# Attention and feed-forward kernel: 64-bit weight words rebuilt by three VectorE steps instead of four, with a scaled copy in an output bank

## The chip, the cores and the metric

The kernel runs on one core of one Trainium2 chip. The metric is the device time in microseconds of one execution; lower is better. Three runs of the kernel before gave 979.25, 982.62 and 982.91 us (median 982.62). A separate execution was taken with the hardware profiler; the views of the trace come from that one.

The engines are called as the profile calls them: PE is TensorE (matrix products), PEld its weight load, DVE is VectorE, ACT is ScalarE, POOL is GpSimd, SP is the engine that issues the DMA transfers. SBUF is the on-chip working memory, PSUM the memory into which PE accumulates.

## The reference

Two stages. The first is attention with a mask from hashes, over 4 batches of 8 heads, 768 positions and 64 dimensions. A position's hash is six bits, the signs of its product with `proj`; a query sees the keys of its own bucket. The second is a feed-forward layer over 3072 tokens, 512 wide inside and out, 2048 in the middle.

```python
q_bits = (np.einsum('bhsd,dk->bhsk', q, proj) > 0)
k_bits = (np.einsum('bhsd,dk->bhsk', k, proj) > 0)
mask = q_bucket[:, :, :, None] == k_bucket[:, :, None, :]
scores = np.where(mask, scale * np.matmul(q, k.transpose(0, 1, 3, 2)), -1000000000.0)
attn = np.exp(scores - np.max(scores, axis=-1, keepdims=True))
attn = attn / (np.sum(attn, axis=-1, keepdims=True) + 1e-09)
x = np.matmul(attn, v)              # then heads side by side: 3072 x 512
h = x @ w_in
g = np.where(h >= 1, h, np.where(h <= -1, 0.0, (h + 1) ** 2 / 4))
out = g @ w_out
```

The two weight matrices come as 64-bit floats. The kernel sees each number as two 32-bit words, a high one (sign, 11 exponent bits, 20 bits of the fraction) and a low one, and makes a 32-bit float of them on the chip.

## The kernel before, in words

**Precision.** Most products are made from a rounded high part and a low part (the difference), so that one product of the reference is three on PE. Names end in `h`/`hi` and `l`/`lo`.

**Attention: heads and units.** The 32 heads are worked through one behind the other in 384 *units* `g` (loop at line 614), twelve to a head (`NU`): two halves of the queries (`hf`) by six blocks of keys (`j`). In what follows a unit is counted within its head, 0 to 11; unit 12 is unit 0 of the next head. Heads go in pairs; an *even* head is the first of its pair, an *odd* one the second. Unit `g` issues, in this order:

- `s_unit(g)`: two products of 384 columns into one of four `s` banks of PSUM (lines 372, 373), then two exponentials on ACT: the rounded one into `ph` (381) and the full one (386), which goes back into the `s` bank, or into `pf` in SBUF where POOL will read it.
- in every second unit, `max_red` (line 315): DVE reduces the two `smax` banks, 768 numbers, to a maximum. There is one pair of such banks, so the next maximum's products wait for the reduce before.
- `lo_unit(g - 1)`: the low part `pl`, full less rounded (line 39, by the helper `sub`): on POOL for blocks 0 and 3, on DVE for the other four.
- `pv_unit(g - 4)`: three products (405, 407, 409) into the *output bank* `obank[hf]`. The four units of delay (`LAG`) mean that `obank[0]` collects in units 4 to 9 and `obank[1]` in units 10 to 15; ACT then copies the bank out (415). In the other six units a bank is idle.
- after every second unit, `max_mm` (311): two products for the maximum of a later head.
- the unit's *tasks*, from a table that is filled beforehand by `at(unit, function)`. Each engine takes its instructions in the order of issue.

**Tasks of a pair.** They prepare the pair that comes two pairs later: in units 0 to 3 of an even head POOL casts the raw rows (153) and makes their low parts (158, shown as line 39 with `t<-raw,t`), four pieces; DMA moves (`move`) copy parts to the other half of the partitions. In unit 3 POOL clamps the maxima (`max_clamp`, 343, 345), in unit 5 PE transposes them (`max_tr`, 350) and ACT copies them out (355). The hash bits are `bits_mm`, four products (211) per half of the positions into an output bank, ACT's negated copy of a part of them (217), and in the next unit `bits_cmp`, a comparison on DVE (222). They stand in units 7 (`obank[1]`) and 11 (`obank[0]`) of the even head, the third `move` behind the second one's comparison in unit 12, the scaling of the bits on POOL (274) in unit 13. V is cast on ACT in unit 6 and its low parts are made on POOL in units 7 and 9.

**Weights.** 32 slices of 128 x 512 numbers are rebuilt: 24 during attention, one per head from head 3 to head 26, and eight in the feed-forward stage. `WeightSplit.steps` returns a slice's steps, and `conv` puts them into the table of tasks with a list of units. `s0` loads the words. `s1` squares the high word, read as a float, on ACT (69) and takes its lower 27 bits shifted left by three on DVE (70); `s2` ors in the two top bits (74), `s3` the low word shifted right (78); `s4` multiplies with 1 or 0 by a test of the square, which makes tiny numbers zero (82). The units are 7, 9, 13 and 15, so that each head holds, on DVE, line 78 of the head before in its unit 1, line 82 in unit 3, and its own lines 70 and 74 in units 7 and 9. Later steps cast (87 or 89), subtract (39) and store.

**Sums.** In heads 8, 16 and 24 a batch is complete; three small DVE steps (673, 674, 678) prepare its sums in unit 11 of the following odd head and unit 5 of the even head behind.

**Feed-forward** begins near 461 us: for two chunks of 384 tokens, twelve products per step into `h` (966) and nine into `y` (829); then the other six chunks by products of half-size blocks (1061). ACT and DVE make the activation between (788 to 803). The eight remaining weight slices are rebuilt at the start of this stage, by a table of steps (lines 1218 to 1238).

Of the kernel before, what the change touches and what calls it, by code (L numbers as in the profile page):

```python
# [11 lines left out]
F32 = mybir.dt.float32  # L12
# [22 lines left out]
WMIN2 = float(np.array([897 << 20], np.int32).view(np.float32)[0]) ** 2  # L35
# [6 lines left out]
class WeightSplit:  # L42
# [3 lines left out]
    def __init__(self, nc, pool, n):  # L46
        self.nc, self.pool, self.n = nc, pool, n
        sc = pool.tile([P, 2], I32, name="wsc", bufs=1)
        nc.vector.memset(sc[:, 0:1], -0x40000000)
        nc.vector.memset(sc[:, 1:2], 29)  # L50
        self.sc = sc

    def steps(self, src, shape, hi, lo, cp, stage=None, low=None, keep=None):
# [10 lines left out]
        def s1():  # L64
            raw = st["raw"]
            sq = st["sq"] = self.pool.tile([P, n], F32, name="wsq")
            a = st["a"] = self.pool.tile([P, n], I32, name="wa", bufs=1)
            high = raw[:, :, 1].bitcast(F32)
            nc.scalar.activation(out=sq, in_=high, func=AF.Square)
            nc.vector.tensor_scalar(out=a, in0=raw[:, :, 1], scalar1=0x07FFFFFF, scalar2=3,  # L70
                                    op0=ALU.bitwise_and, op1=ALU.logical_shift_left)

        def s2():
            nc.vector.scalar_tensor_tensor(out=st["a"], in0=st["raw"][:, :, 1], scalar=self.sc[:, 0:1],
                                           in1=st["a"], op0=ALU.bitwise_and, op1=ALU.bitwise_or)

        def s3():
            nc.vector.scalar_tensor_tensor(out=st["a"], in0=st["raw"][:, :, 0], scalar=self.sc[:, 1:2],
                                           in1=st["a"], op0=ALU.logical_shift_right, op1=ALU.bitwise_or)

        def s4():
            nc.vector.scalar_tensor_tensor(out=st["sq"], in0=st["sq"], scalar=WMIN2,
                                           in1=st["a"].bitcast(F32), op0=ALU.is_ge, op1=ALU.mult)
# [13 lines left out]
        if stage is None:  # L97
            return [s0, s1, s2, s3, s4, s5, s6] + ([put] if keep is not None else [])
# [5 lines left out]
        return [s0, s1, s2, s3, s4, put], [get, s5, s6]  # L104
# [10 lines left out]
def attention(ctx, tc, wst, T1, T2, qk, v, pj, cv, x_d, s_d, e_d, tasks, shared):  # L115
# [4 lines left out]
    shared["work"], shared["small"] = work, small  # L120
# [450 lines left out]
    for hd in range(NH):  # L571
# [7 lines left out]
        if h == 0 and pr + 2 < NPAIR:  # L579
# [9 lines left out]
            bits_at = ((20, 1), (23, 0)) if pr == 0 else ((8 if pr == 1 else 7, 1), (11, 0))  # L589
# [516 lines left out]
def lsh_attn_ffn(ctx: ExitStack, tc: tile.TileContext, qk, v, pj, cv, w_in, w_out, out):  # L1106
# [49 lines left out]

    def wi_steps(i, cp, stage=None):
# [133 lines left out]
```

## Time and profile before

| | |
|---|---|
| three runs | 979.25, 982.62, 982.91 us |
| the profiled execution, its own time | 979.4 us |
| span of its trace, first to last instruction | 977.6 us |
| mean granted TensorE clock | 1.000 |
| busy share PE, PEld, DVE, ACT, POOL | 98%, 91%, 81%, 70%, 36% |
| DVE busy, 76.9 to 409.7 us (heads 4 to 27) | 312.25 of 332.80 us |
| PE busy, 461 to 969 us | 507.94 of 508.00 us |

How to read it. A busy share is an average over the span. PE's records overlap each other (a product of 384 columns is shown as some 0.34 us long while the next one starts 0.176 us behind it), so a busy PE may still be waiting; what counts is the distance from one start to the next. In the timeline a row has the start in us from the span's beginning, the duration in us, engine, line and operation, output and inputs by the program's names, the shape, how many instructions the row stands for, and in brackets how long the engine had been idle and which instruction released it. In the groups by line a row ends with the busy time in us and the mean duration in ns, then the idle time before them.

### The profile page before, as it was taken

Reading aid. Unit: us, or ns where it says so; the run is one execution under the profiler, and the core shown is the slowest. Engines: PE = TensorE matmul, PEld = TensorE weight load, DVE = VectorE, ACT = ScalarE, POOL = GpSimd, SP = SyncE. Lnnn points to the kernel's source line nnn. Section 1 sums busy time; section 2 is a strip of 40 time slices with the busy share of each in tenths; the row PEclk is TensorE's granted clock in tenths of the full one; section 3 lists DMA queues with packets and bytes.
Section 4 is the critical chain, followed back from the end, with each engine's and each line's share of the span. In section 5 each row is a group of like instructions: output and inputs, shape, how many; then the busy total and the mean of one; then the engine's idle time right before and its main releaser. Section 6 shows DMA issues by size and latency. Waiting matters only on the chain.

```text
span 977.6 us, 15547 instructions
## 1 busy us (share of the span) xinstructions
PE 961.9 (98%) x5050; PEld 890.3 (91%) x5050; DVE 788.3 (81%) x1355; ACT 680.2 (70%) x1481; POOL 354.8 (36%) x422
## 2 busy tenths in 40 slices
PE   8999999999999999999999999999999999999998
PEld 7889999999999999999999998888988888888896
DVE  8779999999999999897898788787776777655554
ACT  7888998989989998987755565455564545544444
POOL 8768887777788877566000000000000000000000
PEclk9999999999999999999999999999999999999999
DMA  5775566677666666635494479976459554454431
GB/s 161 191 183 157 153 170 177 175 191 197 179 167 166 157 175 176 153 114 134 128 335 162 139 227 300 295 241 201 119 160 236 146 183 118 148 154 119 119 87 65
DMA packets 95113, 167.56 MB, mean 171 GB/s; under 512 B 13956, under 2 KB 51960, under 8 KB 95032
## 3 DMA queue, kind: packets, MB, share of 16 engines
q1 hardware_dynamic: 94808, 166.56, 60.7%
q8 instruction: 40, 0.66, 0.3%
q14 instruction: 41, 0.34, 0.1%
q10 hardware_dynamic: 224, 0.00, 0.0%
HBM read 106.13 MB, written 33.87 MB: 143 GB/s over the span
## 4 chain that ended last, share of the span: by engine, by line
PE 86%; DVE 5%; POOL 5%; ACT 1%; issue 1%; DMA 1%; DVEq 0%; POOLq 0%; ACTq 0%
PE y L829 27%; PE h L1061 18%; PE h L966 7%; PE smax L311 6%; PE s L373 5%; PE s L372 5%; PE o L405 5%; PE o L407 5%; PE o L409 5%; POOL t L39 3%; PE o L211 2%; DVE nm L315 2%; DVE pl L39 1%; POOL pl L39 1%; POOL t L153 1%
## 5 line engine op out<-in xcount | busy, mean ns | idle before, releaser
L381 ACT ACTIVATE ph<-s 128x384 fp32r<-128x384 f32 x380 | 188.6, 496 | 41.2 <-PE s L373 36.1
L315 DVE TENSOR_REDUCE nm<-smax 128x1 f32<-128x768 f32 x189 | 179.3, 949 | 22.2 <-PE smax L311 21.0
L39 POOL TENSOR_TENSOR pl<-pf,ph 128x384 fp32r<-128x384 f32 x128 | 134.1, 1052 | 78.8 <-ACT pf L386 78.8
L794 DVE SCALAR_TENSOR_TENSOR t<-t 128x384 f32<-128x384 f32 x128 | 71.2, 557 | 101.0 <-ACT z L789 100.8
L39 DVE TENSOR_TENSOR pl<-s,ph 128x384 fp32r<-128x384 f32 x256 | 135.4, 545 | 10.9 <-ACT s L386 9.0
L372 PE MATMUL s<-t 128*128 128x384 f32 x384 | 132.2, 344 | 0.0
L373 PE MATMUL s<-t 128*128 128x384 f32 x384 | 129.6, 337 | 1.7 <-DMA t<-te 1.7
L409 PE MATMUL o<-pl,va 128*128 128x386 f32 x384 | 130.4, 340 | 0.4 <-DVE pl L39 0.4
L407 PE MATMUL o<-ph,vb 128*128 128x386 f32 x384 | 130.0, 339 | 0.0
L405 PE MATMUL o<-ph,va 128*128 128x386 f32 x384 | 129.9, 338 | 0.0
L386 ACT ACTIVATE s<-s 128x384 f32<-128x384 f32 x252 | 125.5, 498 | 0.0
L829 PE MATMUL y<-t,ghi 128*128 128x512 f32 x384 | 124.7, 395 | 0.0
L311 PE MATMUL smax<-t 128*128 128x384 f32 x378 | 100.1, 346 | 4.5 <-DVE nm L315 4.4
L788 ACT ACTIVATE t<-h,mh 128x384 f32<-128x384 f32 x56 | 32.5, 581 | 82.2 <-PE h L966 43.5
L799 ACT CAST ghi<-z 128x384 fp32r<-128x384 f32 x129 | 65.1, 505 | 30.6 <-DVE z L795 26.9
L789 ACT ACTIVATE z<-t,m 128x384 f32<-128x384 f32 x128 | 79.0, 617 | 4.2
L829 PEld LDWEIGHTS y<-t,ghi 128*128 128x128 f32 x384 | 71.3, 188 | 11.1 <-ACT ghi L799 0.3
L1061 PE MATMUL h<-wbig,t 128*128 128x384 f32 x399 | 81.4, 336 | 0.0
L311 PEld LDWEIGHTS smax<-t 128*128 128x128 f32 x378 | 66.6, 188 | 14.5 <-DVE nm L315 13.7
L1061 PEld LDWEIGHTS h<-wbig,t 128*128 128x128 f32 x399 | 71.6, 188 | 5.2
L788 ACT ACTIVATE t<-wsq,mh 128x384 f32<-128x384 f32 x48 | 29.6, 617 | 66.7 <-DVE wsq L1074 40.4
L829 PE MATMUL y<-t,glo 128*128 128x512 f32 x192 | 76.0, 396 | 0.0
(190 smaller groups left out, 2142.9 us busy)
## 6 DMA issues: line engine op xcount, KB each, us to landing
t<-wc SPq DMA_DIRECT2D x92, 256.0 KB
t<-t SPq DMA_DIRECT2D x60, 384.0 KB
wraw<-wc SPq DMA_DIRECT2D x76, 256.0 KB
raw<-in_qk_dram SPq DMA_DIRECT2D x14, 768.0 KB
wraw<-in_w_in_dram SPq DMA_DIRECT2D x16, 512.0 KB
wraw<-in_w_out_dram SPq DMA_DIRECT2D x16, 512.0 KB
t<-ed SPq DMA_DIRECT2D x36, 192.0 KB
xd<-xs SPq DMA_DIRECT2D x32, 192.5 KB
```

The source lines that it names most:

```text
L39: eng.tensor_tensor(out=out, in0=a, in1=b, op=ALU.subtract)
L311: nc.tensor.matmul(out=smax[hd][:, hf, 0:HS], lhsT=t2[:, 0, h, i * P:(i + 1) * P], rhs=t2[:, 1, h, hf * HS:(hf + 1) * HS], start=True, sto ...
L315: nc.vector.tensor_reduce(out=nmp(hd)[:, i:i + 1], in_=smax[hd][:, :, 0:HS], axis=AX.XY, op=ALU.max, negate=True)
L372: nc.tensor.matmul(out=ps[:, 0:HS], lhsT=t1[:, 1, h, ks], rhs=t1[:, 0, h, sl], start=True, stop=False)
L373: nc.tensor.matmul(out=ps[:, 0:HS], lhsT=t2[:, 1, h, ks], rhs=t2[:, 0, h, sl], start=False, stop=True)
L381: nc.scalar.activation(out=ph[:, 0:HS], in_=ps[:, 0:HS], func=AF.Exp, scale=SCALE)
L386: nc.scalar.activation(out=pf, in_=ps[:, 0:HS], func=AF.Exp, scale=SCALE)
L405: nc.tensor.matmul(out=o, lhsT=wa, rhs=ph, start=(jj == 0), stop=False)
L407: nc.tensor.matmul(out=o, lhsT=wb, rhs=ph, start=False, stop=False)
L409: nc.tensor.matmul(out=o, lhsT=wa, rhs=pl, start=False, stop=(jj == NJ - 1))
L829: nc.tensor.matmul(out=ys[c][m], lhsT=g_[:, m * P:(m + 1) * P], rhs=w, start=(first and k == 0), stop=(last and k == 2))
L1061: nc.tensor.matmul(out=ps, lhsT=w[:, cs], rhs=x, start=(n == 0 and s not in (2, 3, 6)), stop=(n == 5), skip_group_check=True)
```

## The change

`s1` to `s4` become four other steps:

- `tail`: DVE shifts the low word right by 29 into `wa`.
- `rebias`: ACT multiplies the high word, read as a float, by 2^-112, which takes 896 off the exponent; numbers that are too small become zero there. During attention the result goes into `obank[0]`, in the feed-forward stage into the slice's own tile.
- `shifted`: DVE shifts that result left by three and ors in `wa`.
- `signed`: DVE takes the result's sign bit and ors in `wa`; this is the finished number.

Both of DVE's last steps take their shift count or mask from a small tile in SBUF (`self.sc`), as lines 74 and 78 did. During attention the units are 9 (`tail`, then `rebias`), 12 (`shifted`) and 14 (`signed`) instead of 7, 9, 13 and 15; the later steps stay where they were. In units 9 to 14 `obank[0]` is idle. The hash products of the pairs from the fourth on move from units 7 (`obank[1]`) and 11 (`obank[0]`) to units 5 and 7, both into `obank[1]`; with them move the comparison of the second half (unit 12 to 8), the third `move` (12 to 8) and POOL's scaling (13 to 9).

```diff
-WMIN2 = float(np.array([897 << 20], np.int32).view(np.float32)[0]) ** 2
+REBIAS = 2.0 ** -112
...
-        nc.vector.memset(sc[:, 0:1], -0x40000000)
-        nc.vector.memset(sc[:, 1:2], 29)
+        nc.vector.memset(sc[:, 0:1], 3)
+        nc.vector.memset(sc[:, 1:2], -0x80000000)
...
-            nc.scalar.activation(out=sq, in_=high, func=AF.Square)
-            nc.vector.tensor_scalar(out=a, in0=raw[:, :, 1], scalar1=0x07FFFFFF, scalar2=3,
-                                    op0=ALU.bitwise_and, op1=ALU.logical_shift_left)
-
-        def s2():
-            nc.vector.scalar_tensor_tensor(out=st["a"], in0=st["raw"][:, :, 1], scalar=self.sc[:, 0:1],
-                                           in1=st["a"], op0=ALU.bitwise_and, op1=ALU.bitwise_or)
-
-        def s3():
-            nc.vector.scalar_tensor_tensor(out=st["a"], in0=st["raw"][:, :, 0], scalar=self.sc[:, 1:2],
-                                           in1=st["a"], op0=ALU.logical_shift_right, op1=ALU.bitwise_or)
-
-        def s4():
-            nc.vector.scalar_tensor_tensor(out=st["sq"], in0=st["sq"], scalar=WMIN2,
-                                           in1=st["a"].bitcast(F32), op0=ALU.is_ge, op1=ALU.mult)
+            nc.vector.tensor_scalar(out=a, in0=st["raw"][:, :, 0], scalar1=29, scalar2=None,
+                                    op0=ALU.logical_shift_right)
+
+        def rebias():
+            st["sq"] = self.pool.tile([P, n], F32, name="wsq")
+            g = st["g"] = st["sq"] if word is None else word()
+            nc.scalar.activation(out=g, in_=st["raw"][:, :, 1].bitcast(F32), func=AF.Copy, scale=REBIAS)
+
+        def shifted():
+            nc.vector.scalar_tensor_tensor(out=st["a"], in0=st["g"].bitcast(I32), scalar=self.sc[:, 0:1],
+                                           in1=st["a"], op0=ALU.logical_shift_left, op1=ALU.bitwise_or)
+
+        def signed():
+            nc.vector.scalar_tensor_tensor(out=st["sq"].bitcast(I32), in0=st["g"].bitcast(I32),
+                                           scalar=self.sc[:, 1:2], in1=st["a"], op0=ALU.bitwise_and,
+                                           op1=ALU.bitwise_or)
...
-    shared["work"], shared["small"] = work, small
+    shared["work"], shared["small"], shared["word"] = work, small, lambda: obank[0]
...
-            bits_at = ((20, 1), (23, 0)) if pr == 0 else ((8 if pr == 1 else 7, 1), (11, 0))
+            bits_at = (((20, 1), (23, 0)), ((8, 1), (11, 0)))[pr] if pr < 2 else ((5, 1), (7, 1))
...
-        conv((2 * i + 3) * NU, wi_steps(i, nc.scalar), (0, 7, 9, 13, 15, 17, 19, 21))
+        conv((2 * i + 3) * NU, wi_steps(i, nc.scalar), (0, 9, 9, 12, 14, 17, 19, 21))
...
-        conv((4 + 2 * n) * NU, first, (0, 7, 9, 13, 15, 16))
+        conv((4 + 2 * n) * NU, first, (0, 9, 9, 12, 14, 16))
...
-            for fn, m in zip(st, (6, 4, 4, 3, 3)):
+            for fn, m in zip(st, (6, 4, 4, 4, 3)):
```

In the feed-forward stage (last lines of the diff) `tail`, `rebias` and `shifted` stand in the step where line 69, 70 and 74 stood, and `signed` in the next one, where lines 78 and 82 stood.

19 lines of the change are left out of this document (9 added, 10 removed).

## The prediction

> **What bounds the kernel now.** I read the page first, then the chain of waits in order of time, then the timeline of single heads. A time such as +2.1 counts from the start of its head, in us.
>
> ```profile
> span 977.6 us, 15547 instructions
> PE 961.9 (98%) x5050; PEld 890.3 (91%) x5050; DVE 788.3 (81%) x1355; ACT 680.2 (70%) x1481; POOL 354.8 (36%) x422
> 488.50 2.11 PE h L966 x12
> ```
>
> The last row is typical of the chain from 461 us on: twelve products of 384 columns in 2.11 us, 0.176 each, one behind the other. The feed-forward stage runs at PE's pace, and the eight conversions in it are hidden by PE: the 0.8 us or so of DVE that each loses (below) is worth nothing there; without that cover it would be 6 us. What can move is the attention stage, so I look at where heads begin (the first product of unit 0, timeline).
>
> ```profile
> 76.88 0.34 PE L372 MATMUL s<-t 128*128 128x384 f32 x1
> 159.83 0.33 PE L372 MATMUL s<-t 128*128 128x384 f32 x1
> 175.33 0.35 PE L372 MATMUL s<-t 128*128 128x384 f32 x1
> 243.12 0.34 PE L372 MATMUL s<-t 128*128 128x384 f32 x1
> 257.94 0.34 PE L372 MATMUL s<-t 128*128 128x384 f32 x1
> 270.68 0.34 PE L372 MATMUL s<-t 128*128 128x384 f32 x1
> 409.74 0.34 PE L372 MATMUL s<-t 128*128 128x384 f32 x1
> ```
>
> These are heads 4, 10, 11, 16, 17, 18 and 28. Odd head 17 lasts 12.74: its 72 products at 0.176 are 12.67, so it holds no wait to speak of. An even head has eight hash products more, 1.41, so its floor is 14.15 and a pair's 26.89. The twelve pairs of heads 4 to 27, in which the 24 conversions lie, last 332.86 against 322.7: **10.2 us of PE's waits is all that there is to win.** Head 16 lasts 14.82 (0.67 over the floor), head 10 15.50 (1.35 over; heads 18 and 26 are of its kind, with a batch's sums on DVE). Three times 1.35 and eight times about 0.64 leave 1.0 for head 4.
>
> Where head 16 waits, with the end of head 15 before it:
>
> ```profile
> 239.80 0.51 PE L311 MATMUL smax<-t 128*128 128x384 f32 x2
> 240.35 0.96 DVE L315 TENSOR_REDUCE nm<-smax 128x1 f32<-128x768 f32 x1 [0.21 <-PE smax L311]
> 241.22 0.55 DVE L39 TENSOR_TENSOR pl<-s,ph 128x384 fp32r<-128x384 f32 x1
> 241.68 1.02 POOL L39 TENSOR_TENSOR pl<-pf,ph 128x384 fp32r<-128x384 f32 x1 [2.33 <-ACT pf L386]
> 241.69 1.56 DVE L74 SCALAR_TENSOR_TENSOR wa<-wraw,wsc,wa 128x512 int32<-128x512 int32 x1
> 242.64 0.97 POOL L153 CAST t<-raw 128x384 fp32r<-128x384 f32 x1
> 243.17 0.94 DVE L315 TENSOR_REDUCE nm<-smax 128x1 f32<-128x768 f32 x1
> 244.04 1.00 DVE L39 TENSOR_TENSOR pl<-s,ph 128x384 fp32r<-128x384 f32 x2
> 244.17 0.30 PEld L311 LDWEIGHTS smax<-t 128*128 128x128 f32 x2 [0.32 <-DVE nm L315]
> 244.97 0.94 DVE L315 TENSOR_REDUCE nm<-smax 128x1 f32<-128x768 f32 x1
> 245.62 0.51 POOL L153 CAST t<-raw 128x384 fp32r<-128x384 f32 x1
> 246.21 1.35 POOL L39 TENSOR_TENSOR t<-raw,t 128x384 fp32r<-128x384 f32 x1
> 248.39 1.25 DVE L82 SCALAR_TENSOR_TENSOR wsq<-wsq,wa 128x512 f32<-128x512 f32 x1
> 249.06 0.67 POOL L343 TENSOR_SCALAR nm<-nm 128x6 f32<-128x6 f32 x1
> 249.82 0.23 POOL L345 TENSOR_SCALAR nm<-nm 128x6 f32<-128x6 f32 x1
> 250.10 0.08 PEld L350 LDWEIGHTS s<-ident,nm 128*12 128x12 f32 x1 [0.54 <-POOL nm L345]
> ```
>
> Two waits make up the 0.64. In unit 0 the maximum's products wait for DVE's reduce (244.17, some 0.26 of PE's time), and in unit 5 the transposition waits for POOL's clamp (250.10, the other 0.38). (Two low subtractions take 244.04 to 244.97, 0.465 each.) Behind both waits stands one thing: a DVE weight step and a POOL instruction that meet. L74 starts 0.01 behind POOL's subtraction and takes 1.56; POOL's cast beside its end takes 0.97 instead of 0.51.
>
> How late may DVE be? A reduce is ready 0.55 after its products start (239.80 to 240.35). The next products start 1.00 after the reduce does (243.17 to 244.17). They are due every two units, twelve products or 2.11. So a reduce may start 2.11 - 0.55 - 1.00 = **0.56 late**; beyond that PE waits the rest and about 0.1 to restart. In proof: the reduce at 243.17 was ready at 239.80 + 2.11 + 0.55 = 242.46, so it was 0.71 late, 0.15 too much, and 0.15 + 0.1 is the wait of unit 0.
>
> **The change part by part.** Durations by line, minimum, median and maximum, where a row has three:
>
> ```profile
> L70 DVE TENSOR_SCALAR wa<-wraw x32: 416/424/1190, 73.1 to 536.0; 128x512 int32<-128x512 int32 x32
> L74 DVE SCALAR_TENSOR_TENSOR wa<-wraw,wsc,wa x32: 729/754/1572, 75.4 to 536.5; 128x512 int32<-128x512 int32 x32
> L78 DVE SCALAR_TENSOR_TENSOR wa<-wraw,wsc,wa x32: 742/840/923, 79.5 to 539.6; 128x512 int32<-128x512 int32 x32
> L82 DVE SCALAR_TENSOR_TENSOR wsq<-wsq,wa x32: 673/691/1253, 82.1 to 540.4; 128x512 f32<-128x512 f32 x32
> L69 ACT ACTIVATE wsq<-wraw x32: 638/662/677, 72.7 to 535.1; 128x512 f32<-128x512 f32 x32
> L39 DVE TENSOR_TENSOR pl<-s,ph 128x384 fp32r<-128x384 f32 x256 | 135.4, 545 | 10.9 <-ACT s L386 9.0 <-POOL nm L256 1.1
> L274 POOL TENSOR_SCALAR bits<-neg,cvt 32x768 fp32r<-32x768 f32 x13 | 17.9, 1378 | 0.0
> 85.28 2.01 POOL L39 TENSOR_TENSOR pl<-pf,ph 128x384 fp32r<-128x384 f32 x2
> 86.38 1.19 DVE L70 TENSOR_SCALAR wa<-wraw 128x512 int32<-128x512 int32 x1
> 87.50 0.56 DVE L39 TENSOR_TENSOR pl<-s,ph 128x384 fp32r<-128x384 f32 x1
> ```
>
> *The steps.* Four DVE steps (medians 0.42 + 0.75 + 0.84 + 0.69 = 2.71) become three. The new first step is of L70's form: 0.42 alone, but blocked where POOL is at work: the last three rows show it started 0.09 before POOL's second instruction was due and ending 0.28 behind it (87.29 to 87.57), the next DVE start 0.21 behind it. The other two read PSUM and one SBUF tensor, with a scalar from memory. No row has them. Floor: L82's 0.67; ceiling: L78's median beside POOL, 0.84. I take L78's minimum, 0.74, the same operands without POOL, because the subtraction that reads PSUM so stays near 0.545 over 256 instructions beside a busy POOL. The next instruction starts 0.07 to 0.08 before a DVE instruction's end (243.17 + 0.87), so each occupies 0.66. The Trainium skill ("VectorE: DVE Perf Modes", the errata section) gives a PSUM source 62 more fixed cycles than an SBUF source, an estimate of 0.065 us a step; by it the gain below would be 12 x 0.065 = 0.8 us less. No row here has the same step from both memories.
>
> ACT's scaled copy replaces a square of the same shape (0.64 to 0.68) and goes from unit 7 to unit 9; ACT stands idle at times in each head, and its exponentials then run up to 0.2 later at the start of the next head.
>
> *Odd heads, into the even head.* The first step now stands where L74 stood and meets the same POOL subtraction, which starts 0.01 earlier. So it is blocked too, until 242.70, and the reduce starts at 242.91 instead of 243.17: 0.45 late, within 0.56. **The wait of unit 0 goes, 0.26.** What is late next is unit 2: the second step now stands in unit 0, ahead of the reduce of unit 1. That reduce starts at 242.91 + 0.87 + 0.93 (two subtractions) + 0.66 = 245.37, was ready at 242.46 + 2.11 = 244.57 and is 0.80 late: 0.24 too much, with the restart **0.34 of new wait**.
>
> *POOL in the even head.* The cast at 242.64, the subtraction at 246.21 and the clamp at 249.06 were lengthened by L74, L78 and L82 (0.46, 0.34, 0.44). The two PSUM steps leave POOL alone if the subtraction's steady 0.545 is a guide. POOL is then about 1 us sooner at the clamp, against a wait of 0.38: **that wait goes.** A regular even head has 0.34 left of 0.64. Eight of them: 2.4.
>
> *Heads 10, 18, 26.* Two more DVE steps for the sums lie between the reduces (rows below, head 10). The second is 48 elements long like the first and meets POOL; 0.26 earlier I expect it ahead of POOL, so I add 0.27 + 0.23 = 0.5 to the 0.80: wait 0.84 in place of 1.35. Three: 1.5. (If it is blocked as now, 0.92, the wait is 1.5 and 0.2 is lost.) Head 4 keeps about 0.8 of 1.0: 0.2.
>
> ```profile
> 161.19 0.27 DVE L673 SCALAR_TENSOR_TENSOR sm<-em,sm 128x48 f32<-128x48 f32 x1
> 161.49 0.92 DVE L674 TENSOR_SCALAR sm<-sm 128x48 f32<-128x48 f32 x1
> 250.19 0.61 ACT L87 CAST wbig<-wsq 128x512 fp32r<-128x512 f32 x1
> 250.69 0.25 ACT L355 CAST te<-s 12x128 fp32r<-12x128 f32 x1
> ```
>
> *The hash products.* In units 5 and 7 they need POOL's second and fourth low parts. The second ends at 247.56; unit 5 ends where the transposition should start, 250.10 - 0.38 = 249.7. The fourth comes a cast and a subtraction (0.51 + 1.01) behind the clamp: 251.6 now, 1 us sooner then. Unit 7 ends at 243.12 + 40 products (7.04) + four pairs of maximum's products (1.41) + the first hash products (0.70) + 0.34 = 252.6. Free. The compare in unit 6 waits for ACT's negated copy, which is queued behind a cast and a small copy (0.61 and 0.25, the ACT rows above), so for at most 0.9; behind it on DVE is the reduce of unit 7, which is ready only 0.88 + 0.55 = 1.4 after unit 6 begins. The copy out and the DMA move go ahead of SP's later work and hold nothing up. POOL's scaling of the bits (1.38) moves from the odd head into unit 9, ahead of a V subtraction and a low part that PE needs only five units later.
>
> *Even heads, into the odd head.* With the second pair of hash products gone from unit 11, PE gives DVE 0.70 (four products) less time there. In unit 9 the reduce should be on time. The first step then costs between 0.35 (free) and 1.38 + 0.21 = 1.59 (a whole bits scaling); I take 0.85, behind half of it. The next reduce is 0.87 + 0.47 + 0.85 - 2.11 = 0.08 late, the one in unit 1 another 0.87 + 0.93 + 0.66 - 2.11 = 0.35, together 0.43: no wait, but near. For strays I charge 0.05 in twelve heads: 0.6.
>
> *The output bank.* PE's unit 4 waits for the third step. It ends near 245.37 + 0.87 + 0.47 + 0.74 = 247.5; unit 4's accumulation starts at 243.12 + 22 products (3.87) + two pairs of maximum's products (0.70) + 0.34 = 248.0. Spare 0.5.
>
> **The sum.** 2.4 + 1.5 + 0.2 - 0.6 = 3.5 us less. The profiled span 977.6 becomes 974.1, its own time 979.4 (1.8 around the span) 975.9. The median of the three runs is 982.62, 3.2 above the profiled one; taken from that, **979.1**. With 0.67 for the PSUM steps the wait in unit 2 is 0.07 shorter twelve times, a gain of 4.3; with 0.84 it is 0.10 longer, and I charge the odd heads as much again, a gain of 1.1.
>
> **Rivals.** *The first step is not held in the odd heads* (it gets in 0.01 before POOL, or POOL starts later because ACT does). For it: the two start within 0.02. Against: POOL led wherever I looked, and POOL's start comes from PE through ACT as before. Price: the reduce of unit 11 is on time, the one of unit 1 0.35 late, no wait. Then 8 x 0.64, about 0.9 in each of three heads and 0.5 in head 4 come back, some 8.3, less 0.6: 974.9. The Trainium skill ("SBUF — State Buffer", Who interferes with whom) says that whichever of the two starts first holds the shared port for its whole instruction; the rows above agree (1.56 against 0.73), and so its rule speaks for my case as long as POOL starts first.
>
> *Slower: the first step in even heads falls behind a whole POOL instruction.* POOL works there without a pause. From a cost of 0.99 on, the reduce of unit 1 makes PE wait; from 1.34 on the one of unit 11 too. At 1.59: 0.25 + 0.1 in unit 0, then 0.35 + 0.1 in unit 2, 0.8 in each of twelve odd heads, 9.6 against the gain of 4.1: 988.1. Against: POOL's bits scaling should be half done by then.
>
> *The waits only move:* PSUM steps at the ceiling and POOL still in the way of one of them; gain about nothing, 982.6.
>
> **How the numbers follow.** Forecast 0.52, first rival 0.20, slower 0.15, only moved 0.13. A measurement of this kernel can tell about 0.5%, 4.9 us, from no change. Faster by more: the first rival and 0.09 of the forecast's upper end, 0.29. Slower by more: 0.13 of the 0.15. Within: 0.58. The range goes from 974.3, just under the first rival, to 987.0, short of the slower rival's end.
>
> **What would show it.** Right: even heads of about 14.5, the wait on DVE's reduce in unit 2 instead of unit 0, no wait of the transposition for POOL, the first step at about 1.2 to 1.3 in odd heads, PSUM steps at one constant length near 0.74, odd heads still 12.74. Wrong: odd heads over 13.0, PE waiting in unit 4 at the output bank or in unit 7 at the hash products, or PSUM steps above 0.84.

## The result, and the profile after

The changed kernel takes 997.0 us (median of six runs, 993.7 to 999.8) where the kernel before took 979.2 beside it (six runs, 978.8 to 982.9): 1.0168 times as long, with an interval of 1.0148 to 1.0187. The forecast was 979.1 with a range to 987.0. It was wrong, and on the wrong side.

The page of the changed kernel: span, busy times, and the chain that ended last by engine.

```profile
span 996.0 us, 15529 instructions
...
PE 965.4 (97%) x5050; PEld 889.5 (89%) x5050; DVE 782.6 (79%) x1323; ACT 681.6 (68%) x1481; POOL 320.7 (32%) x422
...
PE 70%; DVE 20%; ACT 5%; issue 4%; POOL 1%; DMA 1%; DVEq 0%; ACTq 0%; POOLq 0%
```

The same last line of the kernel before:

```profile
PE 86%; DVE 5%; POOL 5%; ACT 1%; issue 1%; DMA 1%; DVEq 0%; POOLq 0%; ACTq 0%
```

DVE and POOL have less to do than before (782.6 against 788.3, and 320.7 against 354.8). Still DVE's share of the chain goes from 5% to 20%: less work, but more of it in PE's way. POOL's 5%, its work up to the clamp, is down to 1%. (In the changed kernel the lines behind the weight steps that are named here have moved up by two: the reduce is L313, the maximum's products L309, unit 0's first product L370.)

The starts of heads 4, 10, 11, 16, 17, 18 and 28 in the timeline of the changed kernel:

```profile
77.16 0.34 PE L370 MATMUL s<-t 128*128 128x384 f32 x1
...
164.90 0.33 PE L370 MATMUL s<-t 128*128 128x384 f32 x1
...
179.79 0.34 PE L370 MATMUL s<-t 128*128 128x384 f32 x1
...
252.40 0.34 PE L370 MATMUL s<-t 128*128 128x384 f32 x1
...
266.93 0.33 PE L370 MATMUL s<-t 128*128 128x384 f32 x1
...
281.45 0.34 PE L370 MATMUL s<-t 128*128 128x384 f32 x1
...
427.44 0.34 PE L370 MATMUL s<-t 128*128 128x384 f32 x1
```

Even head 16 lasts 14.53 (14.82 before), head 10 14.89 (15.50), odd head 17 14.52 (12.74). Heads 4 to 27 together last 350.28, before 332.86: 17.4 more, out of 18.4 more in the span. The even heads did gain, about 0.3 each and 0.6 with a batch's sums, 4.3 in all. **The twelve odd heads lost 1.81 each, 21.7 in all.**

Where the 1.81 comes from, at the end of head 16 (timeline of the changed kernel, POOL, DVE and the maximum's products):

```profile
265.00 0.97 POOL L272 TENSOR_SCALAR bits<-neg,cvt 32x768 fp32r<-32x768 f32 x1
...
265.55 2.66 DVE L66 TENSOR_SCALAR wa<-wraw 128x512 int32<-128x512 int32 x1
265.94 1.00 POOL L39 TENSOR_TENSOR vb<-vraw,va 128x384 fp32r<-128x384 f32 x1
266.92 1.01 POOL L39 TENSOR_TENSOR pl<-pf,ph 128x384 fp32r<-128x384 f32 x1
268.13 0.94 DVE L313 TENSOR_REDUCE nm<-smax 128x1 f32<-128x768 f32 x1
268.83 1.01 POOL L39 TENSOR_TENSOR pl<-pf,ph 128x384 fp32r<-128x384 f32 x1 [0.91 <-ACT pf L384]
269.13 0.62 PE L309 MATMUL smax<-t 128*128 128x384 f32 x2 [1.16 <-DVE nm L313]
...
270.59 0.94 DVE L313 TENSOR_REDUCE nm<-smax 128x1 f32<-128x768 f32 x1
...
271.58 0.62 PE L309 MATMUL smax<-t 128*128 128x384 f32 x2
```

The first step (L66) starts in the middle of POOL's scaling of the bits and takes 2.66. It ends 0.28 behind the *third* POOL instruction (266.92 + 1.01 = 267.93), after which POOL pauses for 0.91. The reduce of unit 11 behind it starts at 268.13, and PE stands 1.16 at the maximum's products in unit 0 (269.13). In unit 2 it loses a little more: 271.58 is 2.45 behind 269.13, where 2.11 are due. The step takes this long in each of the twelve even heads; the view of the lines has the number of each step (minimum, median, maximum; x8 is the feed-forward stage, x13 the scaling in all heads):

```profile
L66 DVE TENSOR_SCALAR wa<-wraw x32: 418/1266/2668, 75.7 to 554.6; 128x512 int32<-128x512 int32 x32
L75 DVE SCALAR_TENSOR_TENSOR wa<-o,wsc,wa x24: 733/738/745, 79.6 to 415.9; 128x512 int32<-128x512 int32 x24
L79 DVE SCALAR_TENSOR_TENSOR wsq<-o,wsc,wa x24: 733/738/745, 81.7 to 417.9; 128x512 int32<-128x512 int32 x24
L79 DVE SCALAR_TENSOR_TENSOR wsq<-wsq,wsc,wa x8: 743/745/747, 504.2 to 558.3; 128x512 int32<-128x512 int32 x8
L272 POOL TENSOR_SCALAR bits<-neg,cvt x13: 972/974/983, 66.6 to 411.0; 32x768 fp32r<-32x768 f32 x13
```

The smallest weight that the reference makes is 4.5e-8 in size. So no run shows that ACT's scaled copy turns a number that is too small into zero.

### The profile page after: what moved, and what is told of

It reads as the page before. It is cut to its first block, busy times and chain, and to the rows that moved or that the text cites. A ratio compares the mean times of both kernels' runs of the same rounds, so it can differ in the third digit from the quotient of the medians.

```text
span 996.0 us, 15529 instructions
## 1 busy us (share of the span) xinstructions
PE 965.4 (97%) x5050; PEld 889.5 (89%) x5050; DVE 782.6 (79%) x1323; ACT 681.6 (68%) x1481; POOL 320.7 (32%) x422
## 4 chain that ended last, share of the span: by engine, by line
PE 70%; DVE 20%; ACT 5%; issue 4%; POOL 1%; DMA 1%; DVEq 0%; ACTq 0%; POOLq 0%
PE y L827 26%; PE h L1059 18%; PE h L964 7%; DVE nm L313 6%; DVE pl L39 5%; PE smax L309 4%; DVE wa L66 3%; PE s L371 3%; PE s L370 3%; PE o L407 3%; PE o L403 3%; PE o L405 3%; DVE wa L75 2%; ACT ph L379 2%; ACT s L384 1%
## 5 line engine op out<-in xcount | busy, mean ns | idle before, releaser
L313 DVE TENSOR_REDUCE nm<-smax 128x1 f32<-128x768 f32 x189 | 179.6, 950 | 28.4 <-PE smax L309 28.2
L39 POOL TENSOR_TENSOR pl<-pf,ph 128x384 fp32r<-128x384 f32 x128 | 130.5, 1020 | 92.2 <-ACT pf L384 92.2
L370 PE MATMUL s<-t 128*128 128x384 f32 x384 | 131.2, 342 | 0.0
L309 PE MATMUL smax<-t 128*128 128x384 f32 x378 | 101.8, 350 | 19.8 <-DVE nm L313 18.2
L309 PEld LDWEIGHTS smax<-t 128*128 128x128 f32 x378 | 65.2, 188 | 35.7 <-DVE nm L313 34.9
L827 PE MATMUL y<-woh,glo 128*128 128x512 f32 x192 | 75.7, 394 | 0.2
```

Of the source, the lines that this page charges most:

```text
L39: eng.tensor_tensor(out=out, in0=a, in1=b, op=ALU.subtract)
L309: nc.tensor.matmul(out=smax[hd][:, hf, 0:HS], lhsT=t2[:, 0, h, i * P:(i + 1) * P], rhs=t2[:, 1, h, hf * HS:(hf + 1) * HS], start=True, sto ...
L313: nc.vector.tensor_reduce(out=nmp(hd)[:, i:i + 1], in_=smax[hd][:, :, 0:HS], axis=AX.XY, op=ALU.max, negate=True)
L370: nc.tensor.matmul(out=ps[:, 0:HS], lhsT=t1[:, 1, h, ks], rhs=t1[:, 0, h, sl], start=True, stop=False)
L827: nc.tensor.matmul(out=ys[c][m], lhsT=g_[:, m * P:(m + 1) * P], rhs=w, start=(first and k == 0), stop=(last and k == 2))
```

## The experiments

The theory at this point: the first step is held, in the even heads, through three POOL instructions, and nothing else costs time. What holds it was open: POOL running without a pause (then any DVE step there would be held), the hash products' new place, or something about the scaling itself. The rivals were that the two steps from the output bank, or DVE's lack of room around the end of an even head, cost as much. All kernels are compared with the kernel before on the same chip, whose median was 981.1 to 981.9 in these comparisons. The table gathers what the texts below speak of, from the starts of unit 0 and the rows of the first step in each trace: the median length of the eight regular even heads, of the twelve odd heads 5 to 27, the sum of heads 4 to 27 (322.7 without waits), and the first step's median in the even heads.

| kernel | median us | ratio (95%) | even | odd | heads 4-27 | first step |
|---|---|---|---|---|---|---|
| before | 979.2 | | 14.78 | 12.74 | 332.9 | |
| changed | 997.0 | 1.0168 (1.0148-1.0187) | 14.49 | 14.55 | 350.3 | 2.66 |
| first step in unit 7 | 981.1 | 0.9999 (0.9986-1.0012) | 14.49 | 13.13 | 332.7 | 0.90 |
| the same, even heads' slices only | 981.6 | 1.0008 (0.9994-1.0022) | 14.49 | 13.13 | 333.3 | 0.89 |
| scaling in unit 13 | 981.2 | 0.9998 (0.9987-1.0010) | 14.49 | 13.13 | 333.3 | 0.72 |
| before + early hash products | 996.2 | 1.0154 (1.0131-1.0176) | 14.79 | 14.42 | 349.6 | |
| scaling behind V's low parts | 981.6 | 1.0001 (0.9987-1.0014) | 14.48 | 13.13 | 333.4 | 0.72 |
| scaling in 13, extra POOL op, 32 partitions | 999.7 | 1.0188 (1.0161-1.0215) | 14.49 | 14.56 | 350.4 | 2.65 |
| the same, 64 partitions | 997.5 | 1.0159 (1.0138-1.0181) | 14.50 | 14.56 | 350.4 | 2.66 |
| the same, 128 partitions | 981.7 | 1.0005 (0.9990-1.0020) | 14.49 | 13.14 | 333.4 | 0.71 |
| changed, scaling on 128 partitions | 981.1 | 0.9999 (0.9985-1.0012) | 14.48 | 13.15 | 333.5 | 0.71 |
| three steps, words in SBUF | 982.0 | 1.0011 (0.9996-1.0025) | 15.08 | 12.74 | 333.9 | 0.42 |
| changed, first in 7, second in 13 | 977.1 | 0.9956 (0.9940-0.9972) | 14.42 | 12.99 | 329.9 | 0.85 |
| before, transposition in unit 6 | 979.6 | 0.9989 (0.9977-1.0002) | 14.67 | 12.74 | 332.0 | |
| words in SBUF, transposition in 6 | 973.0 | 0.9907 (0.9891-0.9923) | 14.14 | 12.74 | 323.4 | 0.42 |

The sums of heads 4 to 27 tell more than the medians where only a few us are in question. In these 15 traces head 4 starts anywhere between 76.56 and 80.30 us, and head 30 lasts either 11.62 to 11.63 (ten traces) or 12.66 to 12.69 (five). Neither follows the edits, and why they vary is open.

**1. The first step back in unit 7, in all heads.**

```diff
-        conv((2 * i + 3) * NU, wi_steps(i, nc.scalar), (0, 9, 9, 12, 14, 17, 19, 21))
+        conv((2 * i + 3) * NU, wi_steps(i, nc.scalar), (0, 7, 9, 12, 14, 17, 19, 21))
-        conv((4 + 2 * n) * NU, first, (0, 9, 9, 12, 14, 16))
+        conv((4 + 2 * n) * NU, first, (0, 7, 9, 12, 14, 16))
```

> The changed kernel with one edit: the first step (the shift of the low word) stands in unit 7 again in every head; everything else as changed. Theory: nearly all of the 18 us come from this step in even heads, where in unit 9 it is held 2.66 us behind three POOL instructions and makes PE wait 1.46 in unit 0 and 0.34 in unit 2 of each odd head. Then the odd heads come back to 12.74 (12 x 1.8 = 21.6 us), and the even heads lose their 0.34 too, since nothing late enters unit 12: 997.0 - 21.6 - 4 = 971. Rival one (the output bank or the scaled copy on ACT holds DVE or PE): odd heads stay near 14.5 and the time near 997. Rival two (the early hash products and POOL's scaling of the bits in unit 9 are the cost, whatever DVE does): the same, 995 or more.

981.1, ratio 0.9999. The 1.8 is gone, so the place of the first step is what costs the 17 us. But not all goes: the odd heads keep 0.39 over the kernel before, so nothing is won against it, and 971 was 10 too low.

**2. Only the slices of the even heads moved back** (the second of the two lists above alone).

> As the run before, but the first step goes back to unit 7 only for the slices that are rebuilt from even heads on; those of odd heads keep it in unit 9. Theory: the odd heads lose their 1.8 of wait (12.74 again), the even heads keep 0.34 in unit 2, since there the step is still held 1.26 by one POOL subtraction: 997.0 - 21.6 = 975.4. If even and odd first steps shared the blame, the time would stay above 980.

981.6. The loss hangs on the even heads' slices alone; the step that is held by one POOL instruction in the odd heads (1.26) costs the regular even heads nothing that shows (14.49 with it and without). The expected 975.4 was too low for the reason of experiment 1: the odd heads keep 0.39.

**3. POOL's scaling of the bits back in unit 13**, the first step left in unit 9.

```diff
-            at(g + n + (2 if pr else 1), bits_scale, pr + 2, nc.gpsimd if pr else nc.scalar)
+            at(g + ((13 if pr > 1 else n + 2) if pr else n + 1), bits_scale, pr + 2, nc.gpsimd if pr else nc.scalar)
```

> The changed kernel with one edit: POOL's scaling of the hash bits stands in unit 13 again instead of unit 9, so that one POOL instruction less runs without a pause behind unit 9 of even heads. Theory A (DVE's step gets the shared port only when POOL pauses): the step starts at +13.15 as now and is held through V's second low part and the low part of block 9, until about +14.9, 1.75 us; PE waits about 0.6 in unit 0 and 0.34 in unit 2 of odd heads, 0.9 instead of 1.8: about 986. Theory B (it is held only for the POOL instruction that runs when it comes, and the 2.66 belong to the scaling instruction itself): held 0.45 + 0.28, about 0.75; no wait in odd heads: 975.

981.2. The rows at the end of head 16 of this kernel, timeline:

```profile
257.69 2.00 POOL L39 TENSOR_TENSOR vb<-vraw,va 128x384 fp32r<-128x384 f32 x2
...
259.26 0.71 DVE L66 TENSOR_SCALAR wa<-wraw 128x512 int32<-128x512 int32 x1
259.63 1.21 POOL L39 TENSOR_TENSOR pl<-pf,ph 128x384 fp32r<-128x384 f32 x1
```

POOL runs on without a pause here too: two subtractions of V, then a low part. Yet DVE's step is held only to the end of the running one (259.69) and is done 0.28 behind it; it is POOL's next instruction that waits, 1.21 instead of 1.01. So a POOL that is never idle does not hold DVE by that alone. Theory B had the step right (0.75); its time of 975 was 6 too low, because the odd heads keep 0.39 here too.

**4. The kernel before with the hash products early**, its four steps unchanged.

```diff
-            bits_at = ((20, 1), (23, 0)) if pr == 0 else ((8 if pr == 1 else 7, 1), (11, 0))
+            bits_at = (((20, 1), (23, 0)), ((8, 1), (11, 0)))[pr] if pr < 2 else ((5, 1), (7, 1))
```

> The kernel before with only the hash products moved (units 5 and 7, both into the second bank, and with them the comparison, the third move and POOL's scaling). The four old weight steps stay, with the second one, which reads two SBUF tensors, in unit 9. Theory A (a step that needs the shared port is starved by POOL's unbroken run): line 74 is held 2.6 us in even heads, odd heads lose about 1.4 in unit 0: 979 + 12 x 1.4 = 996, less a little in even heads. Theory B (only the single-source step is starved, or only the new steps are at fault): line 74 takes at most 1.6, odd heads gain no wait: 976 to 981.

996.2: this part alone brings the loss. The old second step (L74) takes 2.57 where the new first step took 2.66, in the same company:

```profile
269.13 0.98 POOL L274 TENSOR_SCALAR bits<-neg,cvt 32x768 fp32r<-32x768 f32 x1
...
270.05 2.57 DVE L74 SCALAR_TENSOR_TENSOR wa<-wraw,wsc,wa 128x512 int32<-128x512 int32 x1
270.09 1.00 POOL L39 TENSOR_TENSOR vb<-vraw,va 128x384 fp32r<-128x384 f32 x1
271.06 1.01 POOL L39 TENSOR_TENSOR pl<-pf,ph 128x384 fp32r<-128x384 f32 x1
```

So it went in ten of the twelve even heads (2.53 to 2.58). In heads 18 and 26 it was not held. The rows of DVE and POOL at the end of head 18:

```profile
299.97 0.73 DVE L74 SCALAR_TENSOR_TENSOR wa<-wraw,wsc,wa 128x512 int32<-128x512 int32 x1
300.00 1.56 POOL L39 TENSOR_TENSOR vb<-vraw,va 128x384 fp32r<-128x384 f32 x1
```

Here DVE goes first and POOL waits, and the odd heads behind these two have no wait. By the records L74 stands no differently there: it starts 0.03 to 0.04 ahead of POOL's subtraction in these two heads, and 0.01 to 0.06 ahead of it in the ten that were held. What decides between them is not shown.

**5. The scaling in unit 9, but issued behind V's second low part.**

```diff
+            if pr > 1 and pr + 2 < NPAIR:
+                at(g + 9, bits_scale, pr + 2, nc.gpsimd)
```

(below the lines of `split_v`; the old line keeps the first two pairs.)

> The changed kernel with one edit: in unit 9 of even heads POOL's scaling of the hash bits is issued behind V's second low part instead of ahead of it. POOL has as much to do, without a pause, as in the changed kernel. The first step of DVE comes at +13.15 and now meets the low part, which ends near +13.6. Theory B (the step is held for the running instruction only, unless that is the scaling): held about 0.73 as in the run with the scaling in unit 13, no wait in unit 0 of odd heads, 981. Theory A (any unbroken run of POOL starves the step): 2.6 again, 995 to 997.

981.6, first step 0.72. The same three instructions on POOL in another order, and the hold is gone. What counts is which POOL instruction runs when the step comes.

**6 and 7. The scaling in unit 13, and in its place in unit 9 a POOL instruction that nobody needs**, of the same form and length, on 32 and on 128 partitions.

```diff
+    def pool_only():
+        nc.gpsimd.tensor_scalar(out=dum[0:32], in0=dum[0:32].bitcast(F32), scalar1=duc[0:32, 0:1],
+                                scalar2=duc[0:32, 1:2], op0=ALU.mult, op1=ALU.add)
...
+                at(g + 9, pool_only)
```

> The run with the scaling in unit 13, and in unit 9 of even heads, where the scaling stood, a POOL instruction that nobody needs: the same operation on the same 32 partitions and 768 elements of a tile of its own (extra work that is not part of the reference). If the 2.66 come from POOL's instruction itself and not from what the scaling waits for or who waits for it: 2.66 again, odd heads 14.5, about 997. If they come from its dependences (the comparison, the bits tile): 0.7 and 981.

> As the run before, but the unneeded POOL instruction covers all 128 partitions (extra work). Theory P (an instruction on 32 partitions leaves most of POOL idle, the idle part runs ahead into the next instructions, and the port is not let go between them): with 128 partitions the step is held to the end of the instruction that it meets, 0.7 to 0.9, and the time is 981. Theory F (it is this form, one input and scalars from memory, whatever the partitions): 2.66 again and 997.

999.7 (two runs only) and 981.7. The end of head 16 with 32 partitions:

```profile
267.28 0.97 POOL L278 TENSOR_SCALAR dum<-dum,duc 32x768 fp32r<-32x768 f32 x1
...
267.85 2.64 DVE L66 TENSOR_SCALAR wa<-wraw 128x512 int32<-128x512 int32 x1
268.23 1.00 POOL L39 TENSOR_TENSOR vb<-vraw,va 128x384 fp32r<-128x384 f32 x1
269.20 1.00 POOL L39 TENSOR_TENSOR pl<-pf,ph 128x384 fp32r<-128x384 f32 x1
```

and with 128:

```profile
258.39 1.00 POOL L278 TENSOR_SCALAR dum<-dum,duc 128x768 fp32r<-128x768 f32 x1
...
258.96 0.71 DVE L66 TENSOR_SCALAR wa<-wraw 128x512 int32<-128x512 int32 x1
259.34 1.20 POOL L39 TENSOR_TENSOR vb<-vraw,va 128x384 fp32r<-128x384 f32 x1
...
259.61 0.96 DVE L319 TENSOR_REDUCE nm<-smax 128x1 f32<-128x768 f32 x1
261.06 1.02 DVE L39 TENSOR_TENSOR pl<-s,ph 128x384 fp32r<-128x384 f32 x2 [0.49 <-ACT ph L385]
...
262.66 0.95 DVE L319 TENSOR_REDUCE nm<-smax 128x1 f32<-128x768 f32 x1
```

Both steps start 0.57 after POOL's instruction, which lasts 0.97 and 1.00. With 128 partitions DVE has its turn when it ends and POOL's next one is longer by 0.2. With 32, POOL's next two run at their usual 1.00 and DVE waits for both. Nothing else in the two programs differs, and no other instruction depends on this one. The last three rows of the second block show the other loss, which stays: DVE now stands idle 0.49 for ACT before two low subtractions, and the reduce behind them starts 3.05 after the one before it, where 2.11 are due.

**8. The changed kernel with nothing moved, its scaling on 128 partitions**, and the unneeded instruction again on 64.

```diff
+    bits_c = const.tile([P, S], F32R, name="bits")
+    neg_c = const.tile([P, S], F32, name="neg")
...
-            bits_t[pr] = (small.tile([32, S], F32R, name="bits", bufs=1),
-                          small.tile([32, S], F32, name="neg", bufs=1), {})
+            bits_t[pr] = (bits_c, neg_c, {})
```

> The changed kernel with one edit: the tiles of the hash bits are 128 partitions high, and POOL's scaling in unit 9 works on all 128 of them instead of 32 (the 96 others hold zeros that nobody reads; the same 768 elements in each partition). Nothing is moved. Theory P (the number of partitions of the scaling decides whether the DVE step behind it gets the port back at its end): the first step in the even heads ends about 0.3 behind the scaling and takes about 0.7 instead of 2.65, the odd heads lose 0.38 instead of 1.81, and the 1.43 comes back in each of twelve heads, 17 us: within 2 us of the kernel before. Rival (the number of partitions mattered only for the unneeded instruction of the other two runs, because of something else that it changed there): 997 as the changed kernel, ratio 1.017.

> The run with the unneeded POOL instruction in unit 9 once more, on 64 partitions, between the 32 that gave 1.019 and the 128 that gave 1.0005. If anything short of the full 128 lets POOL's next instructions go ahead of the waiting DVE step, the step takes 2.65 and the time is 998 to 1000; if only the quarter does, the step takes 0.7 and the time is that of the kernel before.

981.1 with the wide scaling, against 997.0 without: the hold of the changed kernel is undone by 96 partitions of zeros.

```profile
259.65 1.00 POOL L273 TENSOR_SCALAR bits<-neg,cvt 128x768 fp32r<-128x768 f32 x1
...
260.23 0.71 DVE L66 TENSOR_SCALAR wa<-wraw 128x512 int32<-128x512 int32 x1
260.61 1.20 POOL L39 TENSOR_TENSOR vb<-vraw,va 128x384 fp32r<-128x384 f32 x1
```

With 64 partitions the hold is back in full (997.5, first step 2.66). So it does not take an instruction as narrow as a quarter: behind one of 32 or of 64 partitions POOL's followers go ahead, behind one of 128 they do not.

**9. The three steps with the words in an SBUF tile**, the hash products in their old units 7 and 11, the steps in the old units 7, 9, 13, 15.

```diff
-            bits_at = (((20, 1), (23, 0)), ((8, 1), (11, 0)))[pr] if pr < 2 else ((5, 1), (7, 1))
+            bits_at = (((20, 1), (23, 0)), ((8, 1), (11, 0)))[pr] if pr < 2 else ((7, 1), (11, 0))
...
-        return ws.steps(wout_v[i], (P, DM, 2), woh[i], wol[i], cp, stage, low, None, None if stage is None else word)
+        return ws.steps(wout_v[i], (P, DM, 2), woh[i], wol[i], cp, stage, low)
...
-        conv((4 + 2 * n) * NU, first, (0, 9, 9, 12, 14, 16))
+        conv((4 + 2 * n) * NU, first, (0, 7, 9, 13, 15, 16))
```

(and the same for the slices of `w_in`.)

> One part of the change alone: three DVE steps and the scaled copy on ACT, but the copy goes into the slice's own SBUF tile instead of the output bank; so the hash products stay in units 7 and 11, and the steps stand in units 7, 9 (copy alone, no DVE step), 13 and 15, where lines 70, 69, 78 and 82 stood or near it. The step that met POOL in unit 9 is the one that is dropped. Theory (what is worth something is the empty unit 9, not PSUM): no wait of the maximum's products in unit 0, the transposition's wait mostly gone, odd heads 12.74: 6 to 9 us under the kernel before, about 973 to 975 beside 981. Rival (PSUM as a source is what pays, since the two steps still meet POOL here): within 2 us of the kernel before.

982.0: no difference, as its rival said. The trace says why. No wait for a reduce is left in heads 5 to 27, but every even head now loses 0.93 at the transposition. The two rows are from the timeline around unit 5 of head 16:

```profile
250.73 0.23 POOL L343 TENSOR_SCALAR nm<-nm 128x6 f32<-128x6 f32 x1
...
251.01 0.28 PE L348 MATMUL s<-ident,nm 128*12 128x128 f32 x1 [0.77 <-POOL nm L343]
```

The wait before was 0.38. PE comes sooner by the 0.25 that it no longer loses in unit 0, and POOL's clamp ends 0.27 later in its head (+7.20 for +6.93): POOL stands idle 0.70 for ACT's `pf` in unit 1, where it had no pause before, and the steps from SBUF still lengthen its cast (0.97 for 0.51) and its last low part (1.34 for 1.02). In the regular even heads more is given back at this wait (0.55) than was won in unit 0 (0.25): they last 15.08 for 14.78. Only the three heads with a batch's sums gain, 0.4 each.

**10 to 12. Three edits at these two waits:** the changed kernel with the first step in unit 7 and the second in 13; the kernel of experiment 9 with the transposition one unit later in even heads; and that edit alone in the kernel before.

```diff
-        conv((4 + 2 * n) * NU, first, (0, 9, 9, 12, 14, 16))
+        conv((4 + 2 * n) * NU, first, (0, 7, 9, 13, 14, 16))
```

(in both lists) for the first, and for the two others

```diff
+            gt += hd > 2 and h == 1
             at(gt, max_tr, hd + 2)
             at(gt, max_put, hd + 2)
```

> The changed kernel with two steps moved in the table of units: the first step back to unit 7, and the second step (the first that reads the output bank) from unit 12 to unit 13, so that it stands behind the reduce of unit 1 instead of ahead of it. Theory: the 0.33 to 0.38 that each head still lost with only the first step moved is the 0.66 of this step ahead of that reduce; behind it, it only delays a subtraction, and the next reduce has 0.56 of room. Then the odd heads 5 to 27 have under 0.1 of wait and the regular even heads under 0.15, the three heads with a batch's sums 0.3 to 0.7, together some 2 to 4 us of wait against 10.2 in the kernel before: about 975, ratio 0.993. Rival: DVE has no room at all in units 0 to 4, and the lateness only goes on to the reduce of unit 3; then the heads lose 0.25 to 0.35 in unit 4, and the time is that of the kernel before within 2 us.

> The kernel with the words in an SBUF tile and the hash products in their old places, with one more edit: in even heads the transposition of the clamped maxima and its copy stand in unit 6 instead of unit 5. In the run without that edit no wait for a reduce was left in heads 5 to 27, and every even head lost 0.90 to 0.96 at the transposition, which waited for POOL's clamp (at +6.97, where POOL's cast and last low part ahead of it were lengthened to 0.97 and 1.34 by the two steps). Theory: that wait is all that eats the gain, and unit 6 is late enough. Then the even heads lose 0 to 0.1, and 12 x 0.9 = 11 us go: about 971, ratio 0.989. Rival: the wait gave DVE and ACT time to catch up, and without it the reduces of units 6 to 10 or the changed turn of the s banks make PE wait for 0.3 or more in each even head: 975 or above.

> The kernel before with that one edit alone: in even heads the transposition and its copy in unit 6. Theory: the eight regular even heads lose their 0.35 to 0.42 at the transposition no longer, while the 0.25 of unit 0 stays, so 3 us less than the kernel before: about 978, ratio 0.997. Rival: as for the run above, the waits reappear in units 6 to 10, or heads change by less than 0.1: no difference.

977.1, 973.0 and 979.6. The first is between theory and rival: the wait of unit 2 goes, and one of 0.10 to 0.17, with 0.1 to restart, comes in unit 4 of heads 5 to 27. The second is faster than the kernel before by 0.9% (ratio 0.9891 to 0.9923); heads 16 and 17 of it last 14.15 and 12.74, their floor:

```profile
240.63 0.34 PE L370 MATMUL s<-t 128*128 128x384 f32 x1
...
254.78 0.34 PE L370 MATMUL s<-t 128*128 128x384 f32 x1
...
267.52 0.34 PE L370 MATMUL s<-t 128*128 128x384 f32 x1
```

The third cannot be told from no change: the later transposition does free 0.38, but PE then waits 0.04 to 0.16 for the reduces of units 6 and 10. So the three steps and the later transposition are each worth nothing that can be told alone, and 8.8 us together (973.0 against 981.8 of the kernel before on the same chip). Expectation and result of the second differ by 2 us; its heads agree with the expectation (323.4 against a floor of 322.7). In its trace head 4 starts at 79.26, 2.4 later than in the kernel before, and head 30 lasts 12.66, 1.0 longer, which are the two places that vary without an edit.

## Why the prediction was wrong, point by point

**The step that failed** is the cost of the first step in the even heads, "between 0.35 (free) and 1.38 + 0.21 = 1.59 (a whole bits scaling); I take 0.85". It is 2.58 (265.55 to the next DVE start at 268.13). The ceiling was no ceiling: it supposed that a held DVE step gets its turn when the POOL instruction in front of it ends, as the rows quoted there show it for a POOL instruction of 128 partitions. None of them has a DVE step that comes during one of 32. (One of these readings was also off: the DVE step at 86.38 came 0.13 behind the start of POOL's second instruction, 86.25, and not 0.09 ahead of it. That it ends 0.28 behind that instruction is right.) The prediction's own sum does the rest. With 2.58 for 0.85 the reduce of unit 11 is 0.87 + 0.47 + 2.58 - 2.11 = 1.81 late, 1.25 over the 0.56 of room, with the restart 1.35; the one of unit 1 adds 0.35 + 0.1. Together 1.80 a head; measured 1.81, a little more of it in unit 0 (1.46) and less in unit 2 (0.34). With the port given back at the end of the running instruction, as in experiments 3, 5, 7 and 8, the step takes 0.70 to 0.73, near the 0.85. So the time at which the step would come was right, and what failed is who is served next.

The slower rival, which had 0.15, named the right engines and the right place, but not what happened. Its condition, the step behind "a whole POOL instruction", did not come about: the step met the scaling when 0.55 of its 0.97 had passed, as the argument against this rival expected. The loss came from the two POOL instructions behind, which no rival considered, and at 1.81 a head for the rival's 0.8. That it had the sign right is partly luck. The Trainium skill ("SBUF — State Buffer", Who interferes with whom) says that whoever issues first has the shared pair for its whole instruction. The hold of 0.71 in experiments 3, 7 and 8 agrees. The 2.66 does not: the step is there from 265.55 on, before the POOL instructions of 265.94 and 266.92, and both are served ahead of it.

**A second term was too small.** "For strays I charge 0.05 in twelve heads: 0.6". With the hold gone (experiments 1 to 3, 5, 7, 8) the odd heads still last 13.13 to 13.15, 0.4 over 12.74, 4.7 in twelve. The sum had the two low subtractions of unit 0 ready when DVE comes; the row of experiment 7 shows 0.49 of idle time for ACT ahead of them. ACT's scaled copy now stands in unit 9 ahead of the exponentials, but that alone does not make them late enough to matter: in experiment 9 it stands there too, with the hash products in their old units, and the odd heads last 12.74. The early hash products alone do not either: behind heads 18 and 26 of experiment 4, which have them without the copy, the odd heads last 12.72 and 12.73. That the two together do it is the reading left, and no run shows it by itself. Of the 0.4, moving the second step behind the reduce takes away 0.14 (13.13 with the first step alone in unit 7, 12.99 with the second in 13). So even without the hold the change would have been "only moved", at 981 to 982: the even heads' 4.3 is what the odd heads give back.

**What was right.** The forecast for the even heads (timeline of the changed kernel, around units 0 to 5 of head 16):

```profile
250.96 1.26 DVE L66 TENSOR_SCALAR wa<-wraw 128x512 int32<-128x512 int32 x1
...
253.28 0.51 PE L309 MATMUL smax<-t 128*128 128x384 f32 x2
...
255.63 0.61 PE L309 MATMUL smax<-t 128*128 128x384 f32 x2
...
257.84 0.51 PE L309 MATMUL smax<-t 128*128 128x384 f32 x2
...
258.99 0.09 PEld L348 LDWEIGHTS s<-ident,nm 128*12 128x12 f32 x1
...
259.09 0.95 PE L209 MATMUL o<-t,pw 128*128 128x384 f32 x4
```

- The first step in the odd heads is held to one POOL instruction's end: 1.26, forecast 1.2 to 1.3, and the wait of unit 0 goes.
- The wait in unit 2: 255.63 is 2.35 behind 253.28 and 257.84 is 2.21 behind that, 0.24 and 0.10 over the 2.11 due. Forecast 0.34 in all. Regular even heads lost 0.34 by the median, heads 10, 18 and 26 0.72 to 0.74 (forecast 0.84), head 4 0.92 (about 0.8).
- The transposition no longer waits for POOL: 258.99 has no idle time, as forecast. The hash products in unit 5 follow at once (259.09).
- The steps from the output bank take 0.733 to 0.745 in all 24 heads (0.74 taken), held by nothing. The estimate from the Trainium skill ("VectorE: DVE Perf Modes", the errata section), 0.065 us more from PSUM, does not show: the third step takes 0.738 from PSUM and 0.745 from SBUF.
- POOL's scaling takes 0.97 instead of the 1.38 that it took behind DVE's steps, so by the old ceiling the step would have been even shorter.
- The output bank held PE up nowhere in heads 5 to 27. In head 4 it did: the first product of unit 4 starts 0.36 late there, which was one of the signs of being wrong. The feed-forward stage is as long as before (519.7 us from the start of unit 11 of the last head to the end; 519.8 before).

Of the 18.4 us in the span, 17.4 lie in heads 4 to 27. Some 0.3 lie before head 4, and about 1.1 in head 30, which holds 1.25 of wait where it held 0.18. Head 30 varies by that much without an edit (experiments 2 to 7 keep 11.62 to 11.63), so this part need not be the change's.

## What to carry to other kernels

Before an instruction is moved beside another engine's work on a shared port, write down which instruction will be running there, how wide it is, and how many follow without a pause: the price may be the followers too, here two, and not only the rest of one. Where two waits in the same stretch depend on the same two engines, removing one sends PE sooner to the other; here neither edit gave anything alone, and both together gave 0.9%. And when a step is moved into what looks like free time, check that the instructions that its engine waits for, here ACT's exponentials, are still as early as before.

## What the runs showed of the hardware that was not expected

- A first step (a shift from SBUF to SBUF) that comes while a POOL instruction of 32 or 64 partitions runs waits for that one and for the two POOL instructions that follow without a pause: it takes 2.64 to 2.68 us. No run has another number of followers. Behind the same instruction on 128 partitions it takes 0.70 to 0.73 and the next POOL instruction waits 0.2. The duration of POOL's instruction is the same, 0.97 to 1.00. Why the width matters is open: theory P of experiment 7 fits what the three widths did, but no run shows the inside of POOL.
- A step with two inputs from SBUF was held in the same way in ten of twelve heads of experiment 4 (2.53 to 2.58), where it came in the last 0.04 to 0.08 us of the scaling. Steps with one input from PSUM were not: they never took above 0.75 beside any POOL work, twelve of them while the scaling on 32 partitions ran (experiment 3); the second step from SBUF in experiment 9 took 0.74 to 1.06.
